# Attention followed by two MLPs on one core: row sums finished on ScalarE, one transfer for the tails of q and of k, and another order of the attention steps

## The chip, the core and the metric

The kernel runs on one core of one Trainium2 chip. A core has five engines with a queue of instructions each: TensorE (PE in the profile, with its weight loads apart as PEld), VectorE (DVE), ScalarE (ACT), GpSimd (POOL) and SyncE (SP), which here only issues transfers. Transfers run on 16 DMA engines beside them. The metric is the device time of one execution in microseconds, lower is better.

## The reference, cut to what matters

Attention comes first, for 4 batches and 8 heads, with 576 positions and 64 numbers a head. Its output, reordered to 2304 tokens of 512 numbers, goes through two MLPs.

```python
scores = scale * np.matmul(q, k.transpose(0, 1, 3, 2))
cum = np.cumsum(np.maximum(s, 0.0), axis=-1)
bias = -(cum[:, :, :, None] - cum[:, :, None, :])
scores = np.where(causal, -1000000000.0, scores + np.minimum(bias, 0.0))
scores = scores - np.max(scores, axis=-1, keepdims=True)
attn = np.exp(scores)
attn = attn / (np.sum(attn, axis=-1, keepdims=True) + 1e-09)
return np.matmul(attn, v).astype(np.float32)
...
h = x @ w_in          # first MLP: 512 -> 2048 -> 512
g = np.maximum(h, 0.0) + alpha * np.minimum(h, 0.0)
return (g @ w_out).astype(np.float32)
...                   # second MLP: the same shapes, r = max(h, 0), g = r * r
```

## The kernel before

**Attention.** The 32 heads are worked in 16 pairs (two heads of one batch). A pair has 576 positions: four blocks of 128 rows for each head (i = 0 to 3), and a tail of 64 rows for each head. The two tails are put together into one block of 128 rows (i = 4), and its scores are cut into two halves of 288 columns, so that the index h in a step's name is a head for i < 4 and a half of the columns for i = 4. A step has a name: `qk_ih` are the score matmuls of block i (PE, into one of three PSUM banks), `red_ih` takes the maximum of each row (DVE, line 410), `exp_ih` the exponential with the row's sum beside it (ACT, line 423), `tr_i` turns the exponentials with matmuls against an identity (PE, line 485, into one of four PSUM banks), `v_tr_i` copies them out (DVE, or ACT for i = 1 and the first half of i = 3), `xa` and `xb` are the products with v (PE, lines 519 and 535, which share a single PSUM bank `ps_x`), `v_xa` and `v_xb` copy these out (ACT).

For a later pair there are `lq`, `lk`, `lv` (SP: loads of q, k, v), `hi` and `lo` (POOL, lines 297 and 302: the split of q and k into two parts for fp32r matmuls), `pp` and `ppt` (PE: turning q and k), `e_` (ACT and DVE: copying them out), `dq` and `dk` (SP: copies into the second operands QM and KH of the score matmuls).

**The row sums.** `fin` (line 427) runs on DVE, in three instructions: the two halves of block 4 are added (line 431, 128 x 1), 1e-9 is added to all ten sums of a row (line 432, 128 x 10), and the reciprocal is taken (line 433). `spr` turns the result on PE (line 438), `v_spr` copies it to `rT` (ACT, line 443), `ds` stores it (SP), `di` loads it back as `iv`, spread over the partitions (SP), and `nrm` multiplies the outputs by it (POOL, lines 463 and 465). `iv` and `rT` have one buffer each.

**The order.** Within attention every engine runs its instructions in the order in which they are written out: `in_order` (line 621) chains them. The order comes from a periodic table, `PIPE` (line 713): an item such as `pp_k0+1` stands for this step of the pair after the current one. An item's place in the table is its time in periods; `RAMP` shifts single items of single pairs, and `WARM` puts matmuls without a use (line 640, 128 x 256) behind some steps of pair 0. All steps of all pairs are sorted by that time and emitted. Pairs 2 to 7 also carry the conversion of six weight blocks (`c1` on ACT, `c2` on DVE, `c3` on POOL, `lw` on SP), pairs 8, 9 and 11 to 14 the split of weights or inputs for the first MLP.

**Loads.** `load_qk` (line 245) loads q or k of a pair in three transfers: the 4 x 128 rows of both heads, and then each head's tail of 64 rows (line 256, one transfer a head).

**Behind attention** comes the first MLP, three passes of 16 blocks, and then the second. The first block's matmuls (`ph`, line 586) are written into the order behind `tr_4b` of pair 15. Behind the attention part a scheduler orders the instructions; that order is the same before and after the change, instruction for instruction, from the first conversion of the MLP on.

Of the kernel before, what the change touches and what calls it, by code (L numbers as in the profile page):

```python
# [19 lines left out]
def attention_then_two_mlps(  # L20
# [393 lines left out]
    def exp(n, i, h):  # L414
# [7 lines left out]
            o, m = pr_of[n, i][:, h * 288 : (h + 1) * 288], nmax[:, 1:2]  # L422
        nc.scalar.activation(o, o, AF.Exp, bias=m, scale=-1.0, accum_out=sums_of[n][:, i, h : h + 1])  # L423

    sD = dr.tile([len(pairs), 2, S], F32, name="sD")

    def fin(n):

        sums = sums_of.pop(n)
        rs = rs_[n % 2][:, 0 : 2 * NT].rearrange("p (i h) -> p i h", h=2)  # L430
        nc.vector.tensor_add(sums[:, 4, 0:1], sums[:, 4, 0:1], sums[:, 4, 1:2])
        nc.vector.tensor_scalar(sums, sums, 1e-9, None, ALU.add)
        nc.vector.reciprocal(rs, sums)

    def rs_turn(n):
# [271 lines left out]
    for x in range(2):  # L707
# [41 lines left out]
    def emit(op, n):  # L749
# [6 lines left out]
        elif what == "lo" and n > 1:  # L756
            lo(n, x, 2)
        elif what[0] == "l" and what != "lo":
            if what == "lv" and n > 1:
                load_v(n)  # L760
            elif what == "lw" and lq and n > 1:
                w_load(*lq.pop(0))
            elif what in ("lq", "lk") and n > 1:
                load_qk(n, "qk".find(what[1]))
        elif what == "pp" and n > 0:
            pp(n, x, h)
        elif what == "ppt" and n > 0:
            pp_tail(n)
        elif what == "dq" and n > 1:
            spread_q(n)  # L770
        elif what == "dk" and n > 0:
            spread_k(n)
        elif what == "ds":
            rs_store(n)
        elif what == "di":
            iv_load(n)
        elif what == "e" and n > 0:
            if a == "qt":
                q_tail(n)
            elif a == "kt":  # L780
                k_tail(n)
            else:
                qk_out(n, x, h, EV.get(op, h))
        elif what == "qk":
            qk(n, int(a[0]), int(a[1]))
        elif what == "red":
            red(n, int(a[0]), int(a[1]))
        elif what == "exp":
            exp(n, int(a[0]), int(a[1]))
        elif what == "tr":  # L790
            lasttr = tr(n, int(a[0]), a[1:] or "a")
        elif what == "xa":
            pv_a(n)
        elif what == "xb":
            lastpv = pv_b(n)
        elif what == "fin":
            fin(n)
        elif what == "spr":
            rs_turn(n)
        elif what == "nrm":  # L800
            norm(n)
        elif what == "c1":
            jobs[n] = job(n) if n > 1 else None
            if jobs[n]:
                jobs[n][0]()
        elif what == "c2":
            if jobs[n]:
                jobs[n][1]()
        elif what == "c3":
            if jobs[n]:  # L810
                jobs[n][2]()
        elif what == "v":
            if a == "xa":
                pv_a_out(n)
            elif a == "xb":
                pv_b_out(n)
            elif a == "spr":
                rs_out(n)
            else:
                i, part = int(a[3]), a[4:] or "a"  # L820
                tr_out(n, i, part, EV.get(op, 0 if (i, part) in ((1, "a"), (3, "a")) else 1))

    early = lasttr = None
    in_order()
    RAMP = {("pp", 1): 0.5, ("e_", 1): 0.5, ("dk", 1): 0.5, ("lk", 4): 0.4}
    WARM = {("qk_10", 0): 2, ("qk_11", 0): 3, ("qk_20", 0): 3, ("qk_21", 0): 3, ("qk_30", 0): 3, ("qk_31", 0): 3, ("qk_40", 0): 3, ("tr_0", 0): 2, ("tr_1", 0): 2, ("qk_41", 0): 2}
    when = []
    for p in range(-5, NP + 4):
        for z, item in enumerate(PIPE):
# [430 lines left out]
```

## Time and profile before

| | us |
| --- | --- |
| median of 3 runs (lowest, highest) | 992.71 (991.17, 992.75) |
| the profiled execution | 989.36 |
| its span, first to last instruction | 987.6 |
| PE busy in the span | 960.0 |
| DVE busy | 788.0 |
| ACT busy | 546.3 |
| POOL busy | 338.2 |

The profiled execution spent 1.8 us outside the span, and it was 3.35 us faster than the median of the three runs. "Busy" counts the time in which an engine had an instruction in work; a PE that is busy is not PE at its peak, since matmuls overlap. The times in the profile's rows are microseconds from the start of the span. Attention takes the first 211 us, the two MLPs the other 776.

### The profile page before, as it was taken

The numbers are of one execution on the slowest core, as the hardware profiler recorded it, in microseconds if no ns is written. First come the engines' busy times: TensorE is split into PE (matmuls) and PEld (weight loads), VectorE is DVE, ScalarE is ACT, GpSimd is POOL, SyncE is SP. The second block draws the span as 40 slices with busy tenths as digits, with TensorE's granted clock in tenths as the row PEclk, the third lists the DMA queues.
The fourth block names the chain that finished last, engine by engine and source line by source line (L and its number), as shares of the span: only waits on it lengthen the run. The fifth ranks groups of instructions, "written<-read, shape, count | busy, mean of one in ns | idle before, by whom it ended". The sixth has DMA issues, their size and how long they took to land.

```text
span 987.6 us, 17771 instructions
## 1 busy us (share of the span) xinstructions
PE 960.0 (97%) x6466; PEld 902.4 (91%) x6466; DVE 788.0 (80%) x1431; ACT 546.3 (55%) x1120; POOL 338.2 (34%) x340
## 2 busy tenths in 40 slices
PE   7999999999999999999999999999899999999998
PEld 6888878878999989999999998999899999999998
DVE  6788888869888787777988868688966889678774
ACT  5888778864555544434644435565444654446442
POOL 6345544325333444444235310353003440034400
PEclk9999999999999999999999999999999999999999
DMA  5676766424434334444564541577554866538374
GB/s 130 165 187 179 193 151 149 100 66 133 128 128 128 119 106 160 149 144 147 183 217 134 177 132 32 199 268 231 209 177 121 305 213 210 177 105 272 130 252 132
DMA packets 108201, 161.39 MB, mean 163 GB/s; under 512 B 32690, under 2 KB 81458, under 8 KB 102738
## 3 DMA queue, kind: packets, MB, share of 16 engines
q1 hardware_dynamic: 107634, 159.89, 51.9%
q8 instruction: 51, 0.84, 0.4%
q10 hardware_dynamic: 480, 0.37, 0.1%
q14 instruction: 36, 0.29, 0.1%
HBM read 121.85 MB, written 30.11 MB: 154 GB/s over the span
## 4 chain that ended last, share of the span: by engine, by line
PE 59%; DVE 13%; issue 4%; ACT 2%; POOL 1%; DMA 0%; ACTq 0%; DVEq 0%; POOLq 0%
PE acc L1119 16%; PE ph L586 13%; PE po L867 12%; PE b L989 5%; PE a L989 5%; PE c L989 5%; PE d L989 3%; DVE gg L605 2%; DVE gg L606 2%; ACT gs L608 1%; DVE wo_lo L562 1%; DVE cv_t L119 1%; DVE gs L609 1%; DVE wi_lo L562 1%; DVE xc L904 1%
## 5 line engine op out<-in xcount | busy, mean ns | idle before, releaser
L586 PE MATMUL ph<-xs,wi_hi 128*128 128x384 f32 x768 | 196.6, 335 | 2.4 <-DVE gg L606 1.7
L1119 PE MATMUL acc<-w2s,th 128*128 128x256 f32 x1512 | 185.3, 283 | 6.1 <-ACT th L903 3.7
L1119 PEld LDWEIGHTS acc<-w2s,th 128*128 128x128 f32 x1512 | 183.4, 192 | 7.4 <-ACT th L903 4.1
L867 PE MATMUL po<-gs,wo_hi 128*128 128x512 f32 (+1 forms) x768 | 167.0, 336 | 1.6 <-DVE xT L282 1.1
L586 PEld LDWEIGHTS ph<-xs,wi_hi 128*128 128x128 f32 x768 | 135.9, 188 | 6.2 <-DVE gg L606 3.1
L867 PEld LDWEIGHTS po<-gs,wo_hi 128*128 128x128 f32 x768 | 121.2, 188 | 16.2 <-DVE xT L282 1.3
L586 PE MATMUL ph<-xs,wi_lo 128*128 128x384 f32 x384 | 128.4, 334 | 0.0
L903 ACT CAST th<-g 128x768 fp32r<-128x768 f32 x84 | 69.8, 835 | 73.9 <-PE acc L1119 55.2
L608 ACT CAST gs<-gg 128x768 fp32r<-128x768 f32 (+1 forms) x48 | 39.8, 829 | 124.3 <-DVE gg L606 124.3
L904 DVE TENSOR_TENSOR th<-g,th 128x768 fp32r<-128x768 f32 x84 | 82.0, 984 | 25.1 <-ACT th L903 25.1
L867 PE MATMUL po<-gs,wo_lo 128*128 128x256 f32 (+1 forms) x384 | 99.5, 336 | 0.0
L124 POOL TENSOR_TENSOR wc<-cv_t,wc 128x512 uint32<-128x512 uint32 x32 | 47.0, 1476 | 143.1 <-DVE cv_t L120 95.2
L904 DVE TENSOR_TENSOR w1h<-w1f,w1h 128x512 fp32r<-128x512 f32 (+1 forms) x96 | 70.6, 742 | 24.0 <-ACT w1h L903 23.3
L1000 POOL TENSOR_TENSOR g<-g 128x384 f32<-128x384 f32 x24 | 21.6, 900 | 173.3 <-ACT g L999 168.7
L423 ACT ACTIVATE pr<-pr,nmax 128x128 f32<-128x128 f32 (+3 forms) x128 | 71.9, 562 | 16.0 <-DVE nmax L410 15.7
L609 DVE TENSOR_TENSOR gs<-gg,gs 128x768 fp32r<-128x768 f32 (+1 forms) x48 | 49.0, 1021 | 36.9 <-ACT gs L608 36.9
L903 ACT CAST w1h<-w1f 128x512 fp32r<-128x512 f32 (+1 forms) x96 | 53.7, 565 | 39.0 <-PE b L989 21.4
L605 DVE TENSOR_SCALAR gg<-ph,alpha_sb 128x384 f32<-128x384 f32 x95 | 58.0, 611 | 17.9 <-PE ph L586 17.4
L586 PEld LDWEIGHTS ph<-xs,wi_lo 128*128 128x128 f32 x384 | 72.1, 188 | 0.1
L124 POOL TENSOR_TENSOR wf<-cv_t,wf 128x512 uint32<-128x512 uint32 x32 | 46.7, 1462 | 63.0 <-DVE cv_t L120 63.0
L410 DVE CUSTOM_DVE_ANT_0 pr<-ps_sc,mask 128x128 f32<-128x128 f32 (+3 forms) x128 | 58.9, 480 | 11.5 <-PE ps_sc L384 9.2
L867 PEld LDWEIGHTS po<-gs,wo_lo 128*128 128x128 f32 x384 | 59.4, 188 | 7.7
(162 smaller groups left out, 2026.9 us busy)
## 6 DMA issues: line engine op xcount, KB each, us to landing
w2s<-w2D SPq DMA_DIRECT2D x42, 1024.0 KB
w1f<-w1D SPq DMA_DIRECT2D x72, 256.0 KB
raw_w<-in_moe_w_in_dram SPq DMA_DIRECT2D x32, 512.0 KB
w2D<-whl SPq DMA_DIRECT2D x16, 896.0 KB
raw_w<-in_moe_w_out_dram SPq DMA_DIRECT2D x24, 512.0 KB
w1D<-wc SPq DMA_DIRECT2D x8, 896.0 KB
iv<-sD SPq DMA_DIRECT2D x32, 144.0 KB
raw_q<-in_q_dram SPq DMA_DIRECT2D x16, 256.0 KB
```

The costliest lines, as they stand in the source:

```text
L124: nc.gpsimd.tensor_tensor(d, tt, d, ALU.add)
L410: nc.vector.tensor_tensor_reduce(o, banks.pop(("s", i, h))[:, :w], m, -1.0, first, ALU.add, ALU.min, nmax[:, h : h + 1])
L423: nc.scalar.activation(o, o, AF.Exp, bias=m, scale=-1.0, accum_out=sums_of[n][:, i, h : h + 1])
L586: nc.tensor.matmul(ph[h][:, :HT], ws[a][:, kb * P : (kb + 1) * P], xs[kb][:, bb, h * HT : (h + 1) * HT], start=(cnt == 0), stop=(cnt == 3 ...
L605: nc.vector.tensor_scalar(x, ph[h][:, :HT], 0.0, alpha_sb[:, f : f + 1], ALU.min, ALU.mult)
L608: act = nc.scalar.copy(z[:, 0], a)
L609: sub = nc.vector.tensor_sub(z[:, 1], a, z[:, 0].bitcast(F32))
L867: nc.tensor.matmul(acc, ws[a][:, m * P : (m + 1) * P], gs[:, bb, c_], start=first_ and z == 0, stop=lst and z == 2, skip_group_check=True,)
L903: a = nc.scalar.copy(dst[:, 0], src)
L904: v = nc.vector.tensor_sub(dst[:, 1], src, dst[:, 0].bitcast(F32))
L989: nc.tensor.matmul(pt[:, :HT], hl[:, a, c0 + kb * P : c0 + (kb + 1) * P], xc[i][:, b, kb, :], start=(first and cnt == 0), stop=(cnt == 5), ...
L1119: nc.tensor.matmul(acc[tb // 2][:, (tb % 2) * 256 : (tb % 2 + 1) * 256], th[:, x, qq, tb * P : (tb + 1) * P], ws[:, y, (2 * q + qq) % 4, : ...
```

## The change

Four things change.

- `fin` keeps the two additions, but on ScalarE: two activations of the function Identity, with the second summand given as the bias (a 128 x 1 operand). The constant 1e-9 stands in a tile of its own, `eps`, written once by POOL. The reciprocal becomes a step of its own, `rec`, on DVE.
- `load_qk` loads both heads' tails in one transfer with 128 partitions instead of two with 64.
- The table `PIPE` is another one: the same items, and `rec`, in another order and partly for other pairs (`nrm-3` for `nrm-4`, `di-2` for `di-3`, `lw+2` for `lw+1`).
- `RAMP` holds shifts for some 100 items of pairs 0 to 4, and `WARM` asks for 11 matmuls without a use instead of 26.

```diff
-        for h in range(2):
-            e.dma_start(r[h * TAIL : (h + 1) * TAIL, 8, :], src[h, 4 * P : S])
+        e.dma_start(r[:, 8, :], src[:, 4 * P : S])
...
+    eps = apool.tile([P, 1], F32, name="eps", bufs=1)
+    nc.gpsimd.memset(eps, 1e-9)
...
     def fin(n):
+
+        sums = sums_of[n]
+        nc.scalar.activation(sums[:, 4, 0:1], sums[:, 4, 0:1], AF.Identity, bias=sums[:, 4, 1:2])
+        nc.scalar.activation(sums, sums, AF.Identity, bias=eps)
+
+    def recip(n):
 
         sums = sums_of.pop(n)
         rs = rs_[n % 2][:, 0 : 2 * NT].rearrange("p (i h) -> p i h", h=2)
-        nc.vector.tensor_add(sums[:, 4, 0:1], sums[:, 4, 0:1], sums[:, 4, 1:2])
-        nc.vector.tensor_scalar(sums, sums, 1e-9, None, ALU.add)
         nc.vector.reciprocal(rs, sums)
...
-        "qk_00+0 pp_k0+1 e_q1+1 red_41-1 qk_01+0 lw+1 red_00+0 tr_3a-1 e_k0+1 "
+        "qk_00+0 exp_41-1 tr_2b-1 lv+0 pp_k0+1 red_00+0 hi_q+2 v_tr_2b-1 qk_01+0 "
...
-    RAMP = {("pp", 1): 0.5, ("e_", 1): 0.5, ("dk", 1): 0.5, ("lk", 4): 0.4}
-    WARM = {("qk_10", 0): 2, ("qk_11", 0): 3, ("qk_20", 0): 3, ("qk_21", 0): 3, ("qk_30", 0): 3, ("qk_31", 0): 3, ("qk_40", 0): 3, ("tr_0", 0): 2, ("tr_1", 0): 2, ("qk_41", 0): 2}
...
+    WARM = {("qk_20", 0): 2, ("qk_21", 0): 2, ("qk_30", 0): 2, ("qk_31", 0): 2, ("qk_40", 0): 1, ("tr_0", 0): 1, ("tr_1", 0): 1}
```

Three places show how the instructions move. Rows of the order give line, operation, what is written and read, and the size; numbers behind a name tell buffers apart, and later lines stand a few numbers further down in the changed file.

First the row sums of a pair in the middle. Before, on DVE (`ISA` is the row maximum, whose second instruction reads it out; QS, KS and ptl are copies out of PSUM):

```order
L282 CAST KS_128<-ps_tr 128x512
L345 TENSOR_SCALAR QS_126<-ps_tr 128x2x64
L282 COPY ptl_133<-ps_tr 128x4x128
L410 ISA pr,nmax<-ps_sc,mask 128x128
L410 ISA nmax 128x1
L431 TENSOR_TENSOR sums<-sums 128x1
L432 TENSOR_SCALAR sums<-sums 128x10
L433 RECIPROCAL rs_134<-sums 128x10
L410 ISA pr,nmax<-ps_sc,mask 128x256
```

After, on ACT (the last exponentials of the pair, the copy of k for the next pair, and behind it the two additions):

```order
L422 ACTIVATE pr,sums<-pr,nmax 128x512
L422 ACTIVATE prl,sums<-prl,nmax 128x288 x2
L278 CAST KS_128<-ps_tr 128x512
L431 ACTIVATE sums<-sums 128x1
L432 ACTIVATE sums<-sums,eps 128x10
L278 COPY xT_85<-ps_xb 128x192
L422 ACTIVATE pr,sums<-pr,nmax 128x128 x2
```

The additions have left DVE, where only the reciprocal stays; on ACT they stand behind the last exponentials that write the sums, ahead of the next pair's first ones.

Second, the loads on SP as the table begins (pair 2 has the buffers raw_q_121 and raw_k_122, pair 3 raw_q_130 and raw_k_131). Before:

```order
L265 DMA raw_v_132<-in_v_dram 64x2x64
L251 DMA raw_k_122<-in_k_dram 128x2x256
L256 DMA raw_k_122<-in_k_dram 64x64 x2
L251 DMA raw_q_121<-in_q_dram 128x2x256
L256 DMA raw_q_121<-in_q_dram 64x64 x2
L251 DMA raw_k_131<-in_k_dram 128x2x256
```

After:

```order
L264 DMA raw_v_132<-in_v_dram 64x2x64
L251 DMA raw_q_121<-in_q_dram 128x2x256
L255 DMA raw_q_121<-in_q_dram 128x1x64
L251 DMA raw_k_122<-in_k_dram 128x2x256
L255 DMA raw_k_122<-in_k_dram 128x1x64
L251 DMA raw_k_131<-in_k_dram 128x2x256
```

q of pair 2 now comes ahead of k, and each tail is one row instead of two.

Third, the end of attention on PE, around the first MLP block (`ph`). Before:

```order
L519 MATMUL ps_xa<-pt,raw_v_132 64x128 x2
L485 MATMUL ps_tr<-ident,prl 128x128 x4
L438 MATMUL ps_tr<-ident,rs_134 128x128
L485 MATMUL ps_tr<-ident,prl 128x128
L586 MATMUL ph<-xs_2490,wi_hi 128x384 x2
```

After, where the block's matmuls end:

```order
L591 MATMUL ph<-xs_3029,wi_hi 128x384 x2
L591 MATMUL ph<-xs_3029,wi_lo 128x384
L443 MATMUL ps_tr<-ident,rs_134 128x128
L540 MATMUL ps_xb<-ptl_133,raw_v_132 64x192 x8
L540 MATMUL ps_xb<-ptl_133,raw_v_132 64x64 x2
```

The turn of pair 15's reciprocals (`spr`) stood ahead of the block's 24 matmuls and now stands behind them, just ahead of `xb`; on ACT the copies `rT` and `v_xa` of pair 15 stand behind the cast `wi_hi` now, where they stood ahead of it.

## Rows read from the trace of the kernel before

**Rows 1.** Windows by stage: busy time (and instructions), TensorE clock, DMA share, GB/s

```profile
core 0: us, PE busy (x) PEld busy (x) DVE busy (x) ACT busy (x) POOL busy (x), PEclk, DMA share, GB/s
...
17.00:38.60 21.60, 17.99 (x143) 16.19 (x141) 12.83 (x45) 14.38 (x41) 10.34 (x11) 0.92 0.59 160
36.40:194.50 158.10, 152.39 (x1302) 130.61 (x1301) 135.64 (x421) 134.23 (x396) 74.57 (x78) 0.99 0.66 162
...
211.00:987.00 776.00, 761.98 (x4844) 733.37 (x4842) 616.80 (x899) 378.19 (x630) 238.91 (x222) 1.00 0.51 167
```

**Rows 2.** Windows of one period each, from `exp_30` to the next pair's

```profile
47.84:59.29 11.45, 11.45 (x102) 9.96 (x101) 9.88 (x33) 10.59 (x32) 5.32 (x5) 1.00 0.73 190
...
95.93:110.18 14.25, 12.45 (x92) 9.92 (x91) 11.07 (x33) 10.41 (x31) 6.82 (x7) 0.88 0.77 195
...
122.22:135.12 12.90, 11.65 (x102) 9.97 (x101) 11.17 (x32) 10.09 (x32) 5.58 (x6) 1.00 0.63 144
```

**Rows 3.** Timeline around one `fin`: start, us, instruction [idle before <-releaser]

```profile
127.44 1.43 POOL L302 TENSOR_TENSOR hl_q<-raw_q,hl_q 128x576 fp32r<-128x576 f32 x1
...
127.89 0.99 DVE L431 TENSOR_TENSOR sums<-sums 128x1 f32<-128x1 f32 x1
...
128.81 1.42 POOL L302 TENSOR_TENSOR hl_k<-raw_k,hl_k 128x576 fp32r<-128x576 f32 x1
...
128.92 1.34 DVE L432 TENSOR_SCALAR sums<-sums 128x10 f32<-128x10 f32 x1
...
130.57 0.33 PE L438 MATMUL ps_tr<-ident,rs 128*128 128x128 f32 x1 [1.25 <-DVE rs L433]
```

**Rows 4.** The tile `sums`: ns min/median/max of its instructions, and who waited

```profile
L431 DVE TENSOR_TENSOR sums<-sums x16: 153/360/991, 30.6 to 209.7; 128x1 f32<-128x1 f32 x16
L432 DVE TENSOR_SCALAR sums<-sums x16: 173/534/1356, 30.8 to 209.9; 128x10 f32<-128x10 f32 x16
L433 DVE RECIPROCAL rs<-sums x16: 216/217/218, 31.1 to 210.1; 128x10 f32<-128x10 f32 x16
...
  PE ps_tr L438: 4.5, 7
```

**Rows 5.** ScalarE's two smallest operations, by their lines: ns min/median/max

```profile
L647 ACT ACTIVATE warm<-warm x1: 202/202/202, 4.3 to 4.3; 1x1 f32<-1x1 f32 x1
...
L443 ACT COPY rT<-ps_tr x16: 238/238/255, 33.9 to 210.8; 10x128 f32<-10x128 f32 x16
```

**Rows 6.** Timeline of the start, POOL

```profile
12.19 1.41 POOL L302 TENSOR_TENSOR hl_k<-raw_k,hl_k 128x576 fp32r<-128x576 f32 x1
...
21.21 0.67 POOL L297 TENSOR_SCALAR hl_q<-raw_q 128x576 fp32r<-128x576 f32 x1 [5.44 <-DMA raw_q<-in_q_dram]
```

**Rows 7.** Timeline of PE: `WARM` matmuls, the stall of the start, one in pair 8

```profile
12.95 0.52 PE L640 MATMUL ps_xa<-iv 128*128 128x256 f32 x3
...
23.93 0.54 PE L312 MATMUL ps_tr<-ident_r,hl_q 128*128 128x128 f32 x4 [3.61 <-POOL hl_q L302]
...
98.99 0.30 PE L384 MATMUL ps_sc<-KH,QM 66*128 66x128 f32 x1 [1.49 <-DMA QM<-QS]
```

**Rows 8.** SP's issues of the tails, ns; transfers from 85.6 to 87.0

```profile
L256 SPq DMA_DIRECT2D raw_q<-in_q_dram x26: 476/762/1531, 21.9 to 168.5; - x26
...
DMA packets 667, 0.17 MB, mean 125 GB/s; under 512 B 656, under 2 KB 667, under 8 KB 667
...
q1 hardware_dynamic: 667, 0.17, 54.0%
```

**Rows 9.** Timeline of the end of attention, ACT and PE

```profile
209.53 0.46 ACT L279 COPY xT<-ps_xa 128x384 f32<-128x384 f32 x1
...
214.90 0.62 ACT L561 CAST wi_hi<-wf 128x512 fp32r<-128x512 f32 x1 [3.80 <-PE ph L586]
...
210.63 0.59 PE L586 MATMUL ph<-xs,wi_hi 128*128 128x384 f32 x2
...
214.97 1.64 PE L535 MATMUL ps_xb<-ptl,raw_v 128*64 128x192 f32 x20
```

More of the change, by code (lines that the diff above doesn't have):

```diff
@@ L797, in emit @@
             fin(n)
+        elif what == "rec":
+            recip(n)
         elif what == "spr":
@@ L824, in attention_then_two_mlps @@
     in_order()
-    RAMP = {("pp", 1): 0.5, ("e_", 1): 0.5, ("dk", 1): 0.5, ("lk", 4): 0.4}
-    WARM = {("qk_10", 0): 2, ("qk_11", 0): 3, ("qk_20", 0): 3, ("qk_21", 0): 3, ("qk_30", 0): 3, ("qk_31", 0): 3, ("qk_40", 0): 3, ("tr_0", 0): 2, ("tr_1", 0): 2, ("qk_41", 0): 2}
+    RAMP = {("qk_10", 0): -0.911, ("qk_11", 0): -0.911, ("red_10", 0): -0.911, ("red_11", 0): -0.911, ("exp_10", 0): -0.911, ("exp_11", 0): -0.911, ("qk_00", 0): -0.964, ("red_00", 0): -0.964, ("qk_01", 0): -0.964, ("red_01", 0): -0.964, ("exp_00", 0): -0.964, ("exp_01", 0): -0.964, ("pp_q0", 2): 0.309, ("pp_q1", 2): 0.309, ("e_q0", 2): 0.309, ("e_q1", 2): 0.309, ("tr_3a", 0): -0.232, ("tr_3b", 0): -0.232, ("v_tr_3a", 0): -0.232, ("v_tr_3b", 0): -0.232, ("pp_k0", 2): 0.185, ("pp_k1", 2): 0.185, ("e_k0", 2): 0.185, ("e_k1", 2): 0.185, ("ppt", 3): -0.16, ("e_qt", 3): -0.182, ("v_xa", 4): -0.203, ("xb", 4): -0.181, ("exp_41", 4): -0.478, ("qk_40", 4): -0.478, ("qk_41", 4): -0.478, ("red_40", 4): -0.478, ("red_41", 4): -0.478, ("exp_40", 4): -0.478, ("qk_20", 4): 0.081, ("red_20", 4): 0.081, ("qk_21", 4): 0.081, ("red_21", 4): 0.081, ("exp_20", 4): 0.081, ("exp_21", 4): 0.081, ("tr_2b", 4): 0.031, ("v_tr_2b", 4): 0.031, ("tr_2a", 4): 0.031, ("v_tr_2a", 4): 0.031, ("e_kt", 3): -0.299, ("pp_k0", 4): -0.261, ("pp_k1", 4): -0.261, ("e_k0", 4): -0.261, ("e_k1", 4): -0.261, ("pp_q0", 4): 0.232, ("pp_q1", 4): 0.232, ("e_q0", 4): 0.232, ("e_q1", 4): 0.232, ("dk", 4): 0.103, ("lq", 3): 0.439, ("tr_2b", 0): -0.116, ("v_tr_2b", 0): -0.116, ("tr_2a", 0): -0.116, ("v_tr_2a", 0): -0.116, ("pp_k0", 1): -0.506, ("pp_k1", 1): -0.506, ("e_k0", 1): -0.506, ("e_k1", 1): -0.506, ("tr_4a", 0): -0.216, ("v_tr_4a", 0): -0.216, ("tr_4b", 0): -0.216, ("v_tr_4b", 0): -0.216, ("qk_10", 1): -0.054, ("qk_11", 1): -0.054, ("red_10", 1): -0.054, ("red_11", 1): -0.054, ("exp_10", 1): -0.054, ("exp_11", 1): -0.054, ("di", 2): -0.214, ("hi_k", 3): -0.711, ("exp_41", 2): -0.016, ("qk_40", 2): -0.016, ("qk_41", 2): -0.016, ("red_40", 2): -0.016, ("red_41", 2): -0.016, ("exp_40", 2): -0.016, ("lk", 2): 0.822, ("lw", 3): 0.44, ("ds", 1): 0.576, ("di", 3): -0.321, ("ppt", 2): 0.09, ("fin", 0): 0.036, ("v_spr", 1): 0.137, ("qk_20", 0): -0.121, ("red_20", 0): -0.121, ("qk_21", 0): -0.121, ("red_21", 0): -0.121, ("exp_20", 0): -0.121, ("exp_21", 0): -0.121, ("qk_10", 4): -0.044, ("qk_11", 4): -0.044, ("red_10", 4): -0.044, ("red_11", 4): -0.044, ("exp_10", 4): -0.044, ("exp_11", 4): -0.044, ("qk_20", 1): -0.084, ("red_20", 1): -0.084, ("qk_21", 1): -0.084, ("red_21", 1): -0.084, ("exp_20", 1): -0.084, ("exp_21", 1): -0.084, ("qk_00", 2): 0.032, ("red_00", 2): 0.032, ("qk_01", 2): 0.032, ("red_01", 2): 0.032, ("exp_00", 2): 0.032, ("exp_01", 2): 0.032, ("e_qt", 2): 0.056, ("ds", 2): 0.204, ("tr_4a", 3): -0.018, ("v_tr_4a", 3): -0.018, ("tr_4b", 3): -0.018, ("v_tr_4b", 3): -0.018, ("tr_2b", 2): 0.086, ("v_tr_2b", 2): 0.086, ("tr_2a", 2): 0.086, ("v_tr_2a", 2): 0.086, ("pp_k0", 3): 0.038, ("pp_k1", 3): 0.038, ("e_k0", 3): 0.038, ("e_k1", 3): 0.038}
```

16 rows, old and new, of the table PIPE are left out of this document.

## The prediction, as it was made before the changed kernel ran

> **What bounds the kernel now.** I read the windows by stage first, then windows of one period each, then the timeline at the places where PE stood still. By stage [rows 1], the two MLPs keep PE busy for 762.0 of 776.0 us, and the change touches nothing there. In attention PE is busy for 152.4 of the 158.1 us between 36.4 and 194.5, while DVE and ACT have 135.6 and 134.2. So attention too is PE's, but with holes, and the holes are all that can be won.
>
> What a period costs without holes is seen in [rows 2]: 11.45 us, in which PE is busy for 11.45 and never idle; ACT has 10.59, DVE 9.88. Other periods are longer, up to 12.90 and 14.25 us, with PE busy for no more than 11.65 and, at the lower clock, 12.45. The thirteen periods of the stretch would take 13 x 11.45 = 148.85 us without holes; they took 158.1. So 9.25 us are holes and lost clock.
>
> What the holes are: in the row sums' timeline [rows 3] the addition of line 431, one number a partition, lasts 0.99 us and ends as POOL's `lo_q` ends (128.88 and 128.87); that of line 432 starts during `lo_k` and ends with it (130.26 and 130.23). Without POOL beside them they take 0.15 and 0.17 us, and up to 0.99 and 1.36 with it [rows 4]. PE then waits 1.25 us for the reciprocal, with all its later work behind that wait, and in attention as a whole 4.5 us in 7 such waits [rows 4]. The period of 14.25 us has another cause: the second operand of the score matmuls, copied by a transfer, came 1.49 us late [rows 7], and behind that the clock fell to half of 2.4 GHz for a while (0.88 of 14.25 us [rows 2], so some 12% or 1.7 us).
>
> The start has a hole of its own: PE stands still for 3.61 us, until POOL has split q of pair 2 [rows 7], which waited 5.44 us for its load [rows 6]. Behind it the clock is at half again (0.92 of 21.6 us [rows 1], 1.7 us).
>
> **The change part by part.**
>
> *Row sums on ScalarE.* DVE loses two instructions a pair, at 0.36 and 0.53 us in the median [rows 4]; POOL's splits cannot stretch what is no longer there. The reciprocal stays on DVE, and its sixteen runs took 216 to 218 ns each, never more [rows 4], where the additions just ahead of it were stretched by POOL; so it isn't one that waits for POOL. What PE waits for in `spr` is then the reciprocal a few DVE steps behind the scores, and in the new table `spr` stands behind `xa`, `tr_0` and `qk_21`, some 2.5 us of PE work later than its operand. I take the 4.5 us as gone. ACT gains two instructions a pair. Nothing in the trace adds such columns on ACT; the nearest rows are an activation of one number, 0.20 us, and a copy of 10 x 128, 0.24 us [rows 5]. I take 0.4 us a pair, with 0.35 and 0.6 as ends (0.6 if the second waits out the first's whole pipeline). In a period with weight conversion that makes 10.59 + 0.4 = 11.0 of 11.45 us: ACT still hides under PE, but barely. What is late next if that cover is gone is the first rival.
>
> *One transfer for the tails.* SP issues two transfers fewer a pair, at 0.48 to 0.76 us each [rows 8]. SP isn't on the path, so this is worth nothing but earlier loads: about 1 us a pair by which `dq`, `lq` and the rest can be issued earlier. It costs nothing on PE, ACT or DVE. The same 128 pieces of 256 bytes are moved. In a stretch with almost nothing but such pieces, 667 of them (656 under 512 bytes) take 54.0% of 16 engines for 1.4 us, which is 18 ns each [rows 8]. Spread evenly that is 8 pieces an engine. The Trainium skill, "DMA: Bandwidth & Descriptors", section "Why a DMA increments its semaphore by 16 and not by 1", speaks against it: a transfer uses the largest number of engines up to 16 that divides the slowest dimension of both sides, and here these are 128 partitions and 2 heads, so 2 engines with 64 pieces each. No run here shows it. By that page each tail would land some 1.0 us later (56 x 18 ns, an estimate); by an even spread nothing changes. The sum takes nothing for it, since q and k are loaded well over half a period ahead of their splits; the price if it counts is the second rival.
>
> *The table.* The instructions of a period stay the same, so PE's 11.45 us stay its floor. I went through the new order of one period with the clean period's durations. Every PE step finds its operands and its PSUM bank at least 0.5 us early: the tightest are `xb` behind ACT's `v_xa` (1.6 us), `tr_2a` behind `exp_21` (1.7 us), and the copies `dq` and `dk`, which are issued some 7 and 6 us ahead of the pair's first scores, where one landed late before. POOL has `nrm` between its two splits now, and waits there for `iv`, with 2.6 us to spare. The 1.49 us and the 1.7 us of clock [rows 2, 7] I count as gone too, but for the new order, for ACT's narrow cover and for the clock I leave 2.5 us of new holes (ends 0 and 6). So the stretch gains 9.25 - 2.5 = **6.75 us**.
>
> *The first pairs.* q of pair 2 is loaded ahead of k and with fewer issues, so its split is ready about 2 us earlier, and `pp_q0` of pair 2 now stands behind all of pair 0's scores on PE. I take the 3.61 us and its 1.7 us of clock as gone. Fifteen `WARM` matmuls go: three of them last 0.52 us, overlapping [rows 7], so 0.12 to 0.17 us each, 1.8 to 2.6 us, of which I take 2.1. That is 7.4 us. Against it: `pp_k0` of pair 1 now stands right behind four small scores of pair 0, where PE is at 12.3 us, and POOL has its operand only at 12.19 + 1.41 = 13.6 us [rows 6]: a new hole of 1.3 us. And the copies for pair 2's scores stand behind three loads on SP and may come 1.2 us late. Remains **4.9 us** (ends 1.5 and 7.4).
>
> *The end.* Pair 15 has no later pair's work beside it. Its turn `spr` moves behind the first MLP block, so the block no longer waits for the reciprocal and for the order around it, which gives about 1 us. But `xb` needs the bank that `v_xa` frees. Before, ACT did that at 209.53, long before `xb` at 214.97 [rows 9]; now it stands behind `wi_hi`, which waits for the block itself (3.80 us of waiting, start 214.90), and behind `rT`. So `xb` starts about 1.1 us later. The normalisation of pairs 14 and 15 on POOL moves back by some 4 us, with the MLP's first weight conversion behind it. I take **-0.5 us** (ends -3 and +2).
>
> The sum against the profiled execution: 989.36 - 6.75 - 4.9 + 0.5 = 978.2 us. The median of the three runs is 3.35 us above that execution, and I carry this over: **981.5 us**.
>
> **The rivals.** *ScalarE takes the place of PE.* For it speaks the 0.45 us that is left in [rows 2]. Where ACT waits for PE inside a period (it does so before `v_spr`) this is used up, and a period would be 12.0 us. In the eight or so periods with a conversion or split that costs 8 x 0.55 = 4.4 us more: 986 us. Against it: outside these periods ACT has over 1 us to spare.
>
> *The tails go through few DMA engines, and these become the bound: slower.* Two engines with 64 pieces each of q and of k have 128 x 18 ns = 2.3 us more a period, beside the 0.66 x 11.45 = 7.6 us that the mean engine has already [rows 1, 8]. That is 9.9 of 11.45, and hidden. From 30 ns a piece on it isn't: 128 x 30 = 3.85, 7.6 + 3.85 = 11.45. At 45 ns a period would be 13.4 us, and over the twelve periods with loads that is 12 x 1.95 = 23 us: 1004 us. It decides against the kernel from about 38 ns (a loss of 1 us a period, which eats the whole gain). Against it: 18 ns is what such pieces take in a dense stretch. The page named above gives the two engines; the pace of one engine is not in its rule.
>
> *The late copy becomes the rule: no change.* Each late landing of QM or KH costs 1.49 us and 1.7 us of clock [rows 2, 7]. In the new table `dk`, which needs the last copy of k on ACT, stands behind `dq`. Were it late in three or four pairs, that is 3.5 x 3.2 = 11 us, the whole gain: 993 us.
>
> *No new holes at all.* With 9.25, 7.4 and +1 the time would be 975 us.
>
> **How the numbers follow.** My forecast has 0.65, with its own range of 977 to 985.5. ScalarE as the bound has 0.14 (986), the late copies 0.07 (993), the DMA engines 0.08 (1004, or from 995 on), no holes 0.06 (975). A range of 976 to 988.5 takes in the forecast, ACT as the bound and part of the last, and leaves out some 0.2. A difference of 0.2%, or 2 us, is about what a measurement of this kernel can tell from no change. Faster by more: 0.65 + 0.14 + 0.06 = 0.85; within it: 0.07; slower: 0.08.
>
> **What would show it.** In the profile of the changed kernel the two additions stand on ACT at about 0.2 us each; PE no longer waits for the reciprocal; periods are 11.5 to 11.8 us; PE has a hole of about 1.3 us at 12 to 14 us and none of 3.6 us behind it; `xb` of pair 15 starts about 1 us behind the end of the first block. Wrong it would be if ACT is busy for the whole of the periods with conversions, if PE's longest waits are for QM, KH or POOL's splits, or if the clock is at half in many periods.

## The result and the profile after

The changed kernel took 980.92 us (median of 4 runs, 979.85 to 981.70), the kernel before 992.73 us beside it. The ratio is 0.9882, with a 95% interval of 0.9865 to 0.9899: faster by 1.2%. The profiled execution took 979.85 us (span 978.1), that of before 989.36 (987.6): 9.5 us less.

By stage (the columns are those of [rows 1]; the second row is the same thirteen periods as 36.40 to 194.50 there, the third and fourth are single periods as in [rows 2]):

```profile
17.00:38.60 21.60, 20.47 (x171) 18.10 (x171) 16.98 (x60) 18.49 (x59) 12.45 (x12) 1.00 0.72 191
31.18:180.60 149.42, 149.15 (x1305) 129.15 (x1304) 121.47 (x395) 133.40 (x423) 75.26 (x78) 1.00 0.67 172
54.61:66.03 11.42, 11.42 (x103) 9.95 (x102) 9.23 (x34) 11.09 (x36) 6.43 (x7) 1.00 0.85 208
111.96:123.40 11.44, 11.44 (x103) 9.91 (x102) 9.19 (x31) 9.92 (x34) 5.64 (x6) 1.00 0.61 159
```

The thirteen periods now take 149.42 us for 158.10, and PE is idle for 0.27 us of them. From pair 7 on a period is 11.44 us and PE is never idle (pairs are counted from 0, as in the names of the steps). ACT has at most 11.09 us of a period. The start has no half clock in this profile (1.00 for 0.92).

The row sums (the columns are those of [rows 4]):

```profile
L431 ACT ACTIVATE sums<-sums x16: 291/296/306, 25.3 to 193.5; 128x1 f32<-128x1 f32 x16
L432 ACT ACTIVATE sums<-sums,eps x16: 303/303/305, 25.6 to 193.8; 128x10 f32<-128x10 f32 x16
L438 DVE RECIPROCAL rs<-sums x16: 207/210/216, 28.2 to 194.2; 128x10 f32<-128x10 f32 x16
...
who waited for it (us, times):
  DVE rs L438: 0.2, 1
```

Their time no longer spreads, and PE, which waited 4.5 us for the reciprocal [rows 4], isn't on the list.

Timeline of the start (start, us, instruction, idle before and its releaser), PE and POOL, beside [rows 6, 7]:

```profile
13.61 0.88 PE L311 MATMUL ps_tr<-ident_r,hl_k 128*128 128x128 f32 x8 [1.01 <-POOL hl_k L301]
...
19.68 0.68 POOL L296 TENSOR_SCALAR hl_q<-raw_q 128x576 fp32r<-128x576 f32 x1 [3.95 <-DMA raw_q<-in_q_dram]
...
19.77 0.50 PE L382 MATMUL ps_sc<-KS,QS 128*128 128x512 f32 x1 [0.69 <-DVE nmax L409]
...
23.45 0.30 PE L383 MATMUL ps_sc<-KH,QM 66*128 66x128 f32 x1 [0.36 <-DMA KH<-cumD]
```

The stall of 3.61 us is gone; the largest holes that PE has instead are the 1.01, the 0.69 and the 0.36 us.

Timeline from the end of attention into the first MLP, beside [rows 9]:

```profile
201.08 0.25 ACT L448 COPY rT<-ps_tr 10x128 f32<-10x128 f32 x1
201.75 1.64 PE L540 MATMUL ps_xb<-ptl,raw_v 128*64 128x192 f32 x20 [0.94 <-ACT xT L278]
...
206.70 1.01 POOL L468 TENSOR_TENSOR xT<-xT,iv 128x384 f32<-128x384 f32 x1 [11.03 <-DMA iv<-sD]
...
212.79 1.02 POOL L468 TENSOR_TENSOR xT<-xT,iv 128x384 f32<-128x384 f32 x1 [4.07 <-DMA iv<-sD]
...
214.33 1.30 POOL L124 TENSOR_TENSOR wf<-cv_t,wf 128x512 uint32<-128x512 uint32 x1
...
215.66 0.43 DVE L119 TENSOR_SCALAR cv_t<-cv_g 128x512 uint32<-128x512 uint32 x1 [3.92 <-POOL wf L124]
...
219.41 0.55 DVE L611 SCALAR_TENSOR_TENSOR gg<-ph,gg 128x384 f32<-128x384 f32 x1
...
220.01 0.62 PE L591 MATMUL ph<-xs,wi_hi 128*128 128x384 f32 x2 [4.21 <-DVE gg L611]
```

This is the new loss, read from below: PE stands still for 4.21 us, because `gg` ends at 219.96; DVE was 3.92 us idle before, until POOL had converted a weight block (214.33); POOL had the normalisation of pair 15 ahead of it (212.79), which waited for `iv`; and `iv` was late because `rT` was (201.08, 4.8 us behind the first block's start; before it was 0.2 us behind it, 210.84 for 210.63). Behind that stall the clock was at half for 3.41 us.

So attention ends 14.35 us earlier (the first MLP block starts at 196.28 for 210.63), and some 4.8 us of that are given back in the MLPs.

### The profile page after: what moved, and what is told of

Same layout as the page of the kernel before. It is cut to its first block, busy times and chain, and to the rows that moved or that the text cites. A ratio compares the mean times of both kernels' runs of the same rounds, so it can differ in the third digit from the quotient of the medians.

```text
span 978.1 us, 17664 instructions
## 1 busy us (share of the span) xinstructions
PE 954.1 (98%) x6451; PEld 899.7 (92%) x6451; DVE 773.7 (79%) x1399; ACT 547.6 (56%) x1152; POOL 339.1 (35%) x341
## 2 busy tenths in 40 slices
DMA packets 107242, 161.39 MB, mean 165 GB/s; under 512 B 31730, under 2 KB 80498, under 8 KB 101778
## 4 chain that ended last, share of the span: by engine, by line
PE 87%; DVE 6%; DMA 3%; SPq 1%; issue 1%; ACT 1%; POOL 0%; ACTq 0%; POOLq 0%; DVEq 0%
PE ph L591 19%; PE po L874 18%; PE acc L1126 16%; PE b L996 5%; PE a L996 5%; PE ps_tr L490 5%; PE c L996 4%; PE ps_xa L524 2%; PE ps_sc L382 2%; PE ps_xb L540 2%; PE d L996 2%; PE ps_sc L383 2%; PE ps_tr L311 2%; PE ps_sc L388 2%; DVE xc L911 1%
## 5 line engine op out<-in xcount | busy, mean ns | idle before, releaser
L409 DVE CUSTOM_DVE_ANT_0 pr<-ps_sc,mask 128x128 f32<-128x128 f32 (+3 forms) x128 | 61.8, 486 | 14.8 <-PE ps_sc L383 11.8
L566 ACT CAST wi_hi<-wf 128x512 fp32r<-128x512 f32 x46 | 28.6, 622 | 78.7 <-PE ph L591 76.1
```

Source lines behind the costliest of these rows:

```text
L409: nc.vector.tensor_tensor_reduce(o, banks.pop(("s", i, h))[:, :w], m, -1.0, first, ALU.add, ALU.min, nmax[:, h : h + 1])
```

## The experiments

They ran in batches beside the kernel before, which took 989.7, 991.0, 991.6 and 992.1 us there, so whole times are compared by their ratio to it. And one thing disturbs whole times: some edits ahead change the order in which the scheduler puts the instructions of the MLPs. In the traces of e3, e4, e11 and e12 the engines run them in the order of the changed kernel; in e1, e2 and e6 to e10 the order is another one, in the second MLP above all. From the last `ph` matmul of the first MLP to the end the kernels with the changed kernel's order took 379.0 to 381.8 us (the kernel before 379.0, the changed kernel itself 379.8 and 381.7 in two profiles), those with another order 374.0 to 378.3. So the whole times of e3 and e4 can be held against the changed kernel's; the other edits are judged by places in the trace. All times below are us from the span's start in the profiled execution; `exp_30` is that of pair 1, block 1 and block 5 are the starts of the first and fifth block of the first MLP.

| kernel | exp_30 | block 1 | block 5 | span | median | ratio to before |
| --- | --- | --- | --- | --- | --- | --- |
| before | 36.40 | 210.63 | 245.33 | 987.6 | | |
| after | 31.18 | 196.28 | 236.31 | 978.1 | 980.92 | 0.9882 (0.9865 to 0.9899) |
| e5, after again | 30.97 | 195.47 | 234.97 | 979.3 | 979.71 | 0.9889 (0.9871 to 0.9907) |
| e1, block behind the turn | 31.16 | 195.77 | 231.42 | 971.3 | 974.11 | 0.9842 (0.9825 to 0.9860) |
| e2, and iv of pair 14 earlier | 31.61 | 196.18 | 229.26 | 972.0 | 974.24 | 0.9843 (0.9826 to 0.9859) |
| e3, additions back on DVE | 31.26 | 198.87 | 239.94 | 983.4 | 982.26 | 0.9929 (0.9911 to 0.9946) |
| e4, two tail transfers | 31.07 | 198.28 | 237.99 | 981.8 | 984.28 | 0.9941 (0.9921 to 0.9961) |
| e11, the same again | 30.80 | 200.13 | 240.81 | 982.2 | 984.00 (1 run) | |
| e12, one more issue a load | 31.64 | 200.50 | 242.63 | 984.3 | 986.04 (1 run) | |
| e6, before, additions on ACT | 36.71 | 208.80 | 243.51 | 983.4 | 983.99 | 0.9938 (0.9920 to 0.9956) |
| e7, before, one tail transfer | 36.66 | 210.30 | 245.00 | 983.2 | 986.20 | 0.9953 (0.9937 to 0.9969) |
| e8, old shifts and WARM | 35.35 | 199.74 | 240.50 | 979.1 | 980.86 | 0.9898 (0.9882 to 0.9914) |
| e9, additions twice | 33.01 | 197.75 | 237.95 | 976.0 | 977.80 (1 run) | |
| e10, no WARM | 32.02 | 196.52 | 236.81 | 975.6 | 977.34 (1 run) | |

e5 is the changed kernel once more, as a control:

> The changed kernel itself, unchanged, beside the experiments, so that they can be compared on one chip. The ratio to the kernel before was 0.9882 on the first chip; if it holds, the two chips differ only by a common factor, and the first MLP block starts again at 196 us of the span (before: 210.6).

The ratio held, and so did the places: block 1 at 195.47, the wait of 0.94 us (`xb`) again, and the stall behind it with 3.95 us (at 218.96) for 4.21.

### The end of attention: e1 and e2

```diff
-        if (op, n) == ("tr_4b", NP - 1):
+        if (op, n) == ("v_xa", NP - 1):
             early = mlp_mm(xs, first[0])
```

e2 has this and `("di", 14): -0.5` in `RAMP`.

> The changed kernel, but the first MLP block's 24 matmuls are written behind the step v_xa of pair 15, not behind tr_4b; so PE turns pair 15's reciprocals ahead of the block, and ACT's rT and v_xa no longer stand behind wi_hi. Theory: the 4.21 us stall of PE at 220 us ends a chain (late rT, late iv, late nrm of pairs 14 and 15 on POOL, late weight conversion on POOL behind them, late wi_hi and gg), and everything in it comes 4.3 us earlier now; the 0.94 us wait of xb goes too, and so does the half clock of 3.4 us behind the stall. 980.9 - 4.2 - 0.9 - 1.7 + 0.5 left in other places = 974.6 us (974 to 977). Rival: the stall is the weights' own loads or the scheduler's order of the MLP and stands whatever pair 15 does: a stall of over 3 us stays behind the second block, and only xb's wait goes: 979.5 to 981.

> As e1, and the load of pair 14's reciprocals (di, on SP) half a period earlier, so that it does not stand behind pair 15's store. Theory that POOL's nrm is the last of the chain: nrm of pair 14 runs some 4 us earlier, that of pair 15 and the conversion behind it 2 to 3 us earlier than in e1, and whatever is left of the stall goes: 974 us, up to 1 us under e1. Rival: with e1 the chain has already run out of the way, and pair 15's own rT and iv decide: same as e1 within 0.5 us.

Timeline of e1, POOL and PE:

```profile
207.62 2.88 POOL L468 TENSOR_TENSOR xT<-xT,iv 128x384 f32<-128x384 f32 x1 [4.33 <-DMA iv<-sD]
...
216.70 0.62 PE L591 MATMUL ph<-xs,wi_hi 128*128 128x384 f32 x2 [2.54 <-DVE gg L611]
```

Timeline of e2, the same:

```profile
204.76 1.02 POOL L468 TENSOR_TENSOR xT<-xT,iv 128x384 f32<-128x384 f32 x1 [3.91 <-DMA iv<-sD]
...
209.43 0.62 PE L591 MATMUL ph<-xs,wi_hi 128*128 128x384 f32 x2 [1.74 <-DVE gg L611]
```

The wait of `xb` is gone in both. With pair 15's normalisation 5.2 us earlier (e1) PE's stall shrinks from 4.21 to 2.54 us, and with it 8.0 us earlier (e2) the stall is gone (the 1.74 us is the shorter wait that stands at 207.18 in the changed kernel with 1.51, and in the kernel before at 220.40). From block 1 to block 5 the kernels took 34.70 (before), 40.03 and 39.50 (after), 35.65 (e1) and 33.08 us (e2). So the chain through `rT`, `iv` and POOL is the cause, and it cost some 5 us. Neither expectation was met whole: in e1 I had expected under 1 us of stall to be left, and in the whole time e2's further 2.2 us are not seen. Both versions beat both kernels, 0.984 of the kernel before, with intervals that end below those of the changed kernel. That e1's whole time lies in the range that I gave is luck, though. At the last `ph` matmul of the first MLP e1 is at 597.34 us, the changed kernel at 598.31 and 597.55 (e5): behind block 5 e1 had given back what it had won (365.92 us from there to that matmul for 362.00 and 362.59, with 1.6 us of waits and 3.4 us of half clock near 334 us), and the rest of its gain lies in the second MLP with its other order, 374.0 us for 379.8 and 381.7. e2 is at 593.73 us there, so it keeps 3.8 to 4.6 us.

### The additions: e3, e6 and e9

e3 puts the two additions back on DVE at the same place of the new table:

```diff
-        nc.scalar.activation(sums[:, 4, 0:1], sums[:, 4, 0:1], AF.Identity, bias=sums[:, 4, 1:2])
-        nc.scalar.activation(sums, sums, AF.Identity, bias=eps)
+        nc.vector.tensor_add(sums[:, 4, 0:1], sums[:, 4, 0:1], sums[:, 4, 1:2])
+        nc.vector.tensor_scalar(sums, sums, 1e-9, None, ALU.add)
```

> The changed kernel with the row sums' two additions back on DVE, at the same place of the new table, and nothing else. Theory A, that POOL's stretching of these additions was what PE paid for: PE waits for the reciprocal again, several waits of 0.5 to 1.2 us, in sum 3 to 4.5 us: 984 to 985.5. Theory B, that the distance of spr from the reciprocal in the new table does it: the additions are stretched again (0.36 and 0.53 us in the median, maxima near 1), but PE waits for the reciprocal for under 0.5 us in sum, and the time is that of the changed kernel within 1 us: 980 to 982. I hold B the likelier.

Timeline of e3 in pair 6, DVE, POOL and PE:

```profile
82.95 1.42 POOL L301 TENSOR_TENSOR hl_q<-raw_q,hl_q 128x576 fp32r<-128x576 f32 x1
...
82.99 1.40 DVE L431 TENSOR_TENSOR sums<-sums 128x1 f32<-128x1 f32 x1 [0.47 <-ACT prl L422]
...
84.94 0.68 DVE L281 CAST KS<-ps_tr 128x512 fp32r<-128x512 f32 x1
...
85.68 0.66 PE L490 MATMUL ps_tr<-ident,prl 128*128 128x128 f32 x4 [1.36 <-DVE KS L281]
```

Neither theory held whole. PE doesn't wait for the reciprocal (so far theory B), but the addition of 128 single numbers again lasts as long as POOL's `lo_q` beside it (84.39 and 84.37), DVE is late with the next copy, and PE waits 1.36 us for the PSUM bank which that copy frees. A second such wait is 0.40 us (at 132.61). Block 1 starts 2.6 to 3.4 us later than in the changed kernel, and the ratio is 0.9929 for 0.9882 and 0.9889, with the same order behind attention. So moving the additions pays in the new table too, and not by the wait for the reciprocal. The two waits for DVE's copy are 1.76 us of it; the rest is spread over several periods and was not traced to a cause.

e6 makes the opposite edit in the kernel before, with the reciprocal right behind the additions.

> The kernel before with the row sums' two additions on ScalarE (and the tile eps), the reciprocal right behind them on DVE; old table, two transfers for the tails. Theory: the 4.5 us that PE waited for the reciprocal in 7 waits go to under 1 us, since nothing is left that POOL stretches; the late copies (1.49 us) and the start's stall (3.61 us) stay. The first MLP block starts 3 to 4.5 us earlier than 210.6. Rival: the reciprocal now waits for ACT, which has the additions behind other exponentials, and DVE and PE stand behind it: the waits go to ACT's account and the block starts within 1 us of 210.6, or later.

In e6 the waits of PE for the reciprocal fell from 4.5 us to a single one of 0.6 us (the tile `sums`, those who waited), but a longer wait appeared in pair 6 (timeline of SP and PE):

```profile
  DVE rs L435: 10.2, 15
...
  PE ps_tr L440: 0.6, 1
```

```profile
79.82 1.15 SPq L457 DMA_DIRECT2D iv<-sD  x2
...
82.19 0.80 SPq L356 DMA_DIRECT2D QM<-QS  x1
...
88.62 0.30 PE L384 MATMUL ps_sc<-KH,QM 66*128 66x128 f32 x1 [2.75 <-DMA QM<-QS]
```

PE waits for QM in four pairs now, 4.4 us in all, for 1.49 us before [rows 7]. In pair 6 PE comes no earlier than before (the scores start at 85.58 for 85.42); the copy is issued 1.55 us later (82.19 for 80.64), behind SP's load of `iv`, which waits for POOL's normalisation (its end 79.79 for 78.25). And DVE now stands still for 10.2 us in 15 waits for the additions on ACT, as the rival had it. So the theory held for PE's waits for the reciprocal and not for the time: block 1 starts only 1.83 us earlier. The rest of the 0.6% lies behind attention, which e6 doesn't edit (from block 1 to the end 774.6 us for 777.0).

e9 does the additions twice in the changed kernel:

```diff
         nc.scalar.activation(sums, sums, AF.Identity, bias=eps)
+        nc.scalar.activation(junk[:, 0:1], sums[:, 4, 0:1], AF.Identity, bias=sums[:, 4, 1:2])
+        nc.scalar.activation(junk, sums.rearrange("p i h -> p (i h)"), AF.Identity, bias=eps)
```

> The changed kernel with the row sums' two additions done twice on ScalarE (the second pair into a tile that nobody reads): ACT gets 0.54 us more a pair (0.30 + 0.30 us, overlapping, as they were measured). Theory, that PE stays the bound and ACT has 0.3 to 1.5 us to spare in nearly every period: the first MLP block starts within 0.7 us of the 195.5 to 196.3 us of the changed kernel's own runs. Rival, the first of the prediction, that ACT is at its limit in the eight or so periods with a conversion: 8 x 0.5 = 4 us later, at 200 us.

Two of its periods, one with a conversion and one without:

```profile
56.43:68.03 11.60, 11.60 (x103) 10.02 (x102) 9.38 (x34) 11.49 (x38) 6.92 (x7) 1.00 0.82 200
147.51:158.94 11.43, 11.43 (x103) 9.91 (x101) 9.40 (x31) 10.74 (x36) 5.67 (x6) 1.00 0.61 157
```

From `exp_30` of pair 1 to that of pair 14 it took 148.78 us, the changed kernel 149.42 and 148.81. So in these periods ACT is not the bound, even with 0.6 us more. Block 1 is 1.5 to 2.3 us later all the same, all of it by pair 1, so that expectation was missed. There PE waits 0.95 us for POOL's split of k (at 24.05) and 1.07 us for DVE's copy (at 29.00). Whether ACT has too little room in the start, or a load was late in this one execution, stays open.

### SP and the tails: e4, e11, e12 and e7

e4 and e11 (the same kernel) have two transfers again in the changed kernel; e7 is the opposite edit in the kernel before:

```diff
-        e.dma_start(r[:, 8, :], src[:, 4 * P : S])
+        for h in range(2):
+            e.dma_start(r[h * TAIL : (h + 1) * TAIL, 8, :], src[h, 4 * P : S])
```

e12 keeps the merged transfer and adds a small one behind it, from memory to memory:

```diff
         e.dma_start(r[:, 8, :], src[:, 4 * P : S])
+        if n > 1:
+            e.dma_start(spare[0, 2 * n + x : 2 * n + x + 1, :], src[0:1, 4 * P : 4 * P + 1])
```

> The changed kernel with two transfers for the tails again, one a head, and nothing else. Theory: the merged transfer saves SP time and costs DMA time that nobody waits for: 980 to 982, and 30 more packets under 512 bytes for each of the 32 loads (31730 + 960 = 32690), if the merged transfer runs on 2 engines and each engine of a transfer leaves one packet of its own. Rival 1, SP's time matters: dq, dk and the loads come up to 1 us later in each pair, PE waits for QM, KH or POOL's splits in several pairs: 983 to 986. Rival 2, the 2 engines cost something: the kernel gets faster by 1 us or more, under 980.

> The kernel of e4 (two transfers for the tails, new table) once more, for a second profile. If the 2.2 us wait for the copy into KH at 83 us belongs to the kernel, it is here again (over 1 us, in the same pair), and the first MLP block starts at 198 us or later; if it was one execution's chance, the block starts at 195.5 to 196.5.

> The changed kernel with the merged tails, and behind each load of q and k from pair 2 on one more transfer of 256 bytes from memory to memory that nobody reads: SP issues as often as with two tails, but the tails still go in one transfer. Theory, that SP's time is what e4 and e11 lost: the copy into KH for pair 7 is issued 3 to 3.7 us ahead of the pair's scores again (with one tail: 4.1 and 5.6 us), PE waits over 1 us for it near 82 us, and the first MLP block starts at 198 us or later. Rival, that the spread of the tails over more DMA engines, with its 30 more packets a load, delays the copies: the wait stays under 0.4 us and the block starts at 195.5 to 196.5 us.

The copy into KH for pair 6 in the timeline, its issue on SP and the wait of PE (the expectation of e12 calls it pair 7; counted from 0 it is pair 6). After:

```profile
76.51 0.55 SPq L365 DMA_DIRECT2D KH<-KS  x1
...
81.12 0.30 PE L383 MATMUL ps_sc<-KH,QM 66*128 66x128 f32 x1 [0.22 <-DMA KH<-cumD]
```

e11, and the window of the period:

```profile
76.63 0.55 SPq L366 DMA_DIRECT2D KH<-KS  x1
...
81.87 0.48 PE L384 MATMUL ps_sc<-KH,QM 66*128 66x128 f32 x1 [1.55 <-DMA KH<-KS]
...
76.50:92.89 16.39, 14.84 (x103) 12.91 (x102) 10.13 (x32) 10.86 (x33) 6.87 (x7) 0.79 0.75 200
```

e12:

```profile
79.28 0.55 SPq L369 DMA_DIRECT2D KH<-KS  x1
...
83.86 0.30 PE L387 MATMUL ps_sc<-KH,QM 66*128 66x128 f32 x1 [2.02 <-DMA KH<-KS]
```

The scores of pair 6 start at 80.59 (after), 80.18 (e5), 80.01 (e11), 80.54 (e4) and 81.54 (e12), so SP issued the copy 4.1, 5.6, 3.4, 3.2 and 2.3 us ahead of them. From issue to use it took 4.6 (after, where the last to land was the other copy into KH, from `cumD`), 5.2 (e11), 5.7 (e4) and 4.6 us (e12). PE waited 2.25 us in e4, 1.55 in e11 with 6.8 us of half clock behind it (0.79 in a period of 16.39 us), 2.02 in e12 with 3.4 us of half clock, and 0.59 in e12 a pair earlier. SP is the reason that the issue comes late: in the period ahead of pair 6 its issues fill 10.0 to 10.8 of 11.4 to 12.1 us in all these kernels, and two tails more add up to 1.1 us. In e12, where the tails stay merged and the number of issues is that of two tails, the copy lands within the same 4.6 us as after and is late by its issue. (e12's small transfers add packets too, about as many as second tails do, but no slower landing is seen with them.) In e4 and e11 part of the wait (0.6 to 1.1 us) is also a slower landing, for which I have no cause. So rival 1 of e4 is right in its cause, though PE's wait comes in one pair and not in several.

The packets tell the engines. The page's line for the changed kernel and for e4:

```profile
DMA packets 107242, 161.39 MB, mean 165 GB/s; under 512 B 31730, under 2 KB 80498, under 8 KB 101778
```

```profile
DMA packets 108203, 161.40 MB, mean 164 GB/s; under 512 B 32691, under 2 KB 81459, under 8 KB 102739
```

961 more for 32 loads is 30 a load. The pieces are the same, 128 a load; what the two traces differ in is 960 packets of 4 bytes. The number fits if each engine of a transfer leaves one small packet more: 2 x 16 for two transfers on 16 engines, and 2 for the merged one on 2 engines; on 16 engines it would leave 16, and the difference would be 512. So, by this count (no trace names the engine of a packet), the merged transfer runs on 2 engines. That is what the rule gives that the prediction took from the Trainium skill ("DMA: Bandwidth & Descriptors", "Why a DMA increments its semaphore by 16 and not by 1"), and the trace agrees with it. A cost of it isn't seen: POOL's split waits for a tail of q three times, 6.6 us in all, and in e4 four times, 7.8 us.

> The kernel before with one transfer for both heads' tails, nothing else. Theory of the prediction, that SP is not on the path: the first MLP block starts within 1 us of 210.6. Rival from e4, that SP's time decides how late the copies into QM and KH land, and when POOL gets q of pair 2: the wait for QM of 1.49 us goes, the start's stall of 3.61 us shrinks by about 1 us, the block starts 2 to 4 us earlier.

In the old table the merged transfer does nothing for attention (block 1 at 210.30 for 210.63), and the late QM of pair 7 (pair 8 in the heading of [rows 7]) stays:

```profile
99.48 0.30 PE L383 MATMUL ps_sc<-KH,QM 66*128 66x128 f32 x1 [1.87 <-DMA QM<-QS]
```

So here the theory held; what is saved in all lies behind attention (772.9 us from block 1 to the end for 777.0).

### The start: e8 and e10

e8 takes `RAMP` and `WARM` of the kernel before, e10 sets `WARM = {}`.

> The changed kernel with RAMP and WARM of the kernel before: the new period, the old start. Theory, that the shifts of the first pairs carry a term of their own: the scores of pair 3 start at 48.5 to 51 us instead of 46.2 (50.0 before), the first MLP block 2.5 to 5 us later than 196.3, all of it by 50 us. Rival: the new table alone (q of pair 2 loaded ahead of k, the merged tails) removes the start's stall, and the shifts are worth under 1 us.

Timeline of e8:

```profile
21.67 0.68 POOL L296 TENSOR_SCALAR hl_q<-raw_q 128x576 fp32r<-128x576 f32 x1 [6.25 <-DMA raw_q<-in_q_dram]
...
23.88 0.67 PE L311 MATMUL ps_tr<-ident_r,hl_q 128*128 128x128 f32 x4 [4.45 <-POOL hl_q L301]
```

With the old shifts the stall of the start is back, longer than before, though the period and the merged tails are new. The scores of pair 3 start at 50.09 (50.00 before, 46.23 after), block 1 3.5 to 4.3 us later than in the changed kernel: the theory held. The thirteen periods take 148.71 us with the old shifts, so the period owes them nothing. In the whole time only 0.001 of the ratio is left; the traces show block 5 5.5 us later than in e5 and the end 0.2 us earlier, so the other order of the MLPs makes up for it.

> The changed kernel without the 11 matmuls of WARM (0.12 to 0.17 us each, 1.3 to 1.9 us). Theory, that they are work on PE's path: the scores of pair 2 start 1.0 to 1.9 us earlier than 34.8 to 35.0 us, and the first MLP block as much earlier than 195.5 to 196.3. Rival 1: PE waits for other engines there anyway, and the waits grow by what the matmuls took: no difference (under 0.4 us). Rival 2: an emptier PE gets half the clock for longer, and the scores of pair 2 start later.

The stretch from 13 to 24 us, in e10, e5 and the changed kernel's first profile (three kernels' windows, one fence each):

```profile
13.00:24.00 11.00, 10.27 (x47) 9.07 (x48) 6.78 (x21) 7.33 (x21) 6.76 (x12) 0.53 0.74 177
```

```profile
13.00:24.00 11.00, 9.96 (x70) 9.49 (x71) 7.71 (x26) 7.84 (x24) 7.13 (x12) 0.84 0.76 182
```

```profile
13.00:24.00 11.00, 8.96 (x68) 8.06 (x68) 7.60 (x24) 7.97 (x24) 6.77 (x12) 1.00 0.73 172
```

As in rival 2: without the eleven matmuls the clock is at half for nearly all of the stretch (10.24 us from 13.47 on), the scores of pair 2 start at 35.89 for 34.84 and 35.05, and block 1 is no earlier. In the nine other profiles with the new shifts the clock was at half there for 0, 3.41 or 6.83 us, so some chance is in it, and e10 is a single profile.

## Why the prediction was right, and where its steps were wrong

The sum was made against the profiled executions. By their marks (the prediction gives the third and fourth together, as 0.5 us lost; its 1 us of gain at the block leaves 1.5 us of loss behind it):

| step | forecast | measured | from |
| --- | --- | --- | --- |
| the first pairs | -4.9 | -5.2 | exp_30 of pair 1: 36.40 to 31.18 |
| thirteen periods | -6.75 | -8.7 | 158.13 to 149.42 |
| from there to the first block | -1 | -0.4 | 16.10 to 15.68 |
| first block to the end | +1.5 | +4.8 | 777.0 to 781.8 |
| sum | -11.15 | -9.5 | 987.6 to 978.1 |

**The periods** were right in their mechanism. Waits for the reciprocal, the late QM and its half clock are gone, and a period is PE's 11.44 us. The allowance of 2.5 us for new holes was too much: 0.6 us is left above 13 x 11.45. Without the moved additions (e3) the thirteen periods take 151.92 us, without the merged tails 151.53 (e4) and 153.65 (e11); the old table with either edit alone takes 155.77 (e6) and 157.60 (e7). So both edits count in the new table. What the table gives by itself no run shows.

**The additions on ScalarE** cost more than I took, 0.54 us a pair for 0.4 (from 193.50, the first's start, to 194.04, the next instruction's), within the ends that I gave. The Trainium skill has the price that the trace of before lacked ("ScalarE: Activation LUTs", "What ACT_TABLE_LOAD costs"): about 280 ns and 0.833 ns a column for an activation whose bias is an operand of 128 x 1, which for 1 and 10 columns would be 281 and 288 ns, an estimate; the trace is near it with 296 and 303 ns. The additions are hidden in the periods, as e9 shows with twice as many. The rival "ScalarE takes the place of PE" is out.

**One transfer for the tails** I valued at nothing, since SP isn't on the path. That step is wrong for the new table: e4, e11 and e12 put 2 to 5 us on it, most of it in one pair, where SP's issues fill nine tenths of a period and a copy of 4.6 us has 4.1 to 5.6 us to land. It holds for the old table (e7). The prediction counted what SP issues fewer, but not how full SP was, and it had `dk` issued some 6 us ahead of the scores. "Late copies become the rule" was thus the rival that the kernel is nearest to; the merged tails keep it away. "Few DMA engines become the bound" had its premise right (2 engines) and its price not: PE waits for none of these loads, and POOL waits for them no longer than with two transfers (6.6 us for q's tails, 7.8 in e4).

**The first pairs** came out at the size that I gave, and the new hole too (1.01 us for 1.3), with a smaller one behind the copies (0.36 for 1.2). e8 shows that the shifts and the shorter `WARM` together carry 4.2 of the 5.2 us. The term for `WARM` alone is open: I took 2.1 us for fifteen matmuls less, by their duration alone; in e10 taking out the other eleven gave nothing, with the clock at half for 10.24 us.

**The end** was mis-sized, the largest miss. The prediction began with the MLPs as a stage that the change doesn't touch, and 4.8 us are lost there. It named the steps (`xb` 1.1 us later; it was 0.94; the normalisation of pairs 14 and 15 some 4 us later with the first weight conversion behind it), but gave the second no price, although PE's work hangs on that conversion. It cost 4.21 us and a stretch of half clock. e1 and e2 show it by shortening and removing that stall. At 4.4 us lost in all, the end lies outside the ends of -3 and +2 that I gave.

That the median came so near, 980.9 for 981.5, is partly luck: the periods came out 2.0 us better than in the sum and the end 3.9 us worse, so that its 978.2 came near the profiled 979.85, and I carried 3.35 us over from profile to median, where it was 1.07.

## What to carry to other kernels

When an order gains time ahead of a seam, follow what else crosses the seam: here the stores, loads and normalisations of the last pairs stood behind a block that had been pulled forward, and gave back a third of the gain. One more shift (e2) kept most of that to the end of the first MLP; the one line of e1 alone lost it again further on. Judge such an edit where it acts and again at the end of the stage, for a later order can add or take as much. An engine that only issues transfers has a share of busy time too, and where its issues fill nine tenths of a period each one saved moves the next copy. An instruction that moves to another engine can make the engine that it left wait for it (e6), so a change of engine and a change of order have to be tried together.

## What the runs showed of the hardware

- A transfer of 256 bytes from memory to memory, 28 times in e12, left 896 packets more (32626 for 31730 under 512 bytes): 32 each, half of 16 bytes and half of 4, so by the count above it too was cut up for 16 engines.
- Eleven matmuls without a use, of 256 columns each, some 1.5 us of work, went with several us less of half clock in the start (from 13 to 24 us 0.53 granted without them, in one profile, and 0.69 to 1.00 with them, in nine).
- An addition of one number a partition on ScalarE took 0.28 to 0.31 us in all pairs (after, e6, e9); on DVE it took 0.15 us where POOL did nothing beside it, and up to 1.40 us where POOL did (before, e3).
